# Value products behind two more product steps, a fourth bank for the first unit, an earlier tile, and a subtraction on another engine

## The chip, the cores and the metric

The kernel runs on one core of a Trainium2 chip. The core has a matrix engine (TensorE, PE in the profile), three engines for elementwise work (VectorE or DVE, ScalarE or ACT, GpSimd or POOL), and SyncE (SP), which only issues DMAs here. Each engine runs its own instructions in order and waits on semaphores for the others. Matrix products land in PSUM, which this kernel uses as eight banks of 128 x 512 fp32. The metric is the device time of one execution in microseconds.

## The reference

The output mixes sliding-window attention and a SwiGLU block, both of the same input, by a gate for each row:

```python
def _A_ref(x, wqkv, wo):                 # x: 1 x 2048 x 512
    H = 32; Dh = 16; W = 256
    q, k, v = split(x @ wqkv)            # 32 heads of 16
    scores = einsum("bhqd,bhkd->bhqk", q, k) * Dh ** -0.5
    mask = (i - j >= 0) & (i - j < W)    # the last 256 keys
    p = softmax(where(mask, scores, -1e9))
    return heads_joined(einsum("bhqk,bhkd->bhqd", p, v)) @ wo
def _B_ref(x, w_gate, w_up, w_down):     # 512 -> 1792 -> 512
    return (silu(x @ w_gate) * (x @ w_up)) @ w_down
g = sigmoid((x * gate_w).sum(-1, keepdims=True))
out = g * _A_ref(x) + (1 - g) * _B_ref(x)
```

## The kernel before

**Precision.** Products of fp32 operands are made of halves: a tensor is split into a high part (a cast to the matrix engine's fp32 format) and a low part (the rest). `split(hi, lo, src, hi_eng, lo_eng)` issues the cast on one engine and the subtraction on another. Three products then make one: high x high, high x low, low x high (`mm3`, lines 80 to 82).

**Stages.** Up to about 165 us the input is split, and the values, queries, keys and the first part of the feed-forward products are made. Then runs the stage of this case, up to about 635 us: attention over eight groups of four heads, with the other feed-forward products dealt in between, so that TensorE has work while the softmax is on its way. From 635 us on comes the last stage: the down projection and the output projection of the attention.

**The dealt products.** A unit is a block of 128 rows of gate or up (`UNITS`), computed in four chunks of 512 tokens, twelve matmuls a chunk. `stream()` is a generator that yields after each step. The first unit goes through `whole` (L506) with one matmul of 128 rows a step. All others go through `lanes` (L527): there one step is two matmuls, one on the upper and one on the lower 64 rows of the array, which run side by side; the lower lane is `LAG` = 18 steps behind. When a chunk is complete, `copy_out` has ScalarE copy its bank to `ev` (L499) and a DMA store it in DRAM (`raws`).

**Banks.** `bank(name)` takes the banks of a name in turn. Each of `pa`, `pb`, `pc`, `pd` has two at first. For this stage `pb0` is added to `pa`, for the dealt products, and `pb1` to `pc`, so `pa` and `pc` have three.

**Attention.** A tick is one head of one block of 128 tokens. In a tick, `stage1` makes the scores of the next group for the row maximum (L560, into `pc`, read by VectorE L562), and `stage2` the transposed scores of this group (L599, into `pd`); ScalarE takes their exponential (L601), and GpSimd cuts the window's edges with two selects (L603, L606). Four blocks are a slot. Once in a slot, in the second tick (`hd == 1`) of its first block (`part == 0`), stand the value products of the slot before: `av` issues 96 matmuls (64 in the first slot of a group) on half the rows each (L621), alternating between two banks, the first from `pc`, the second from `pd`; in the last group both come from `pc`. Behind them, `evacuate` has ScalarE copy the second bank to `ob` (L632), VectorE copy the first to `oe` (L638), GpSimd add them (L639) and store them in DRAM (`od<-oe`, L640). In the last group VectorE does the sum itself (L634), and GpSimd only stores.

**How many steps stand where.** `DEAL` gives the number of steps of each of a slot's four blocks, (4, 9, 9, 8), and (9, 9, 9, 8) in the last group (`t >= g7`, where there is no stage 1). A block's number is dealt out over its four ticks as evenly as whole numbers allow, so the four of the first block are 1, 1, 1, 1. In a tick the order is: the scores, then the value products and `evacuate` if it is their tick, then the steps, then what the table `AT` holds for the end of that tick.

**The table `AT`.** `at(k, f)` has `f` run at the end of tick `k`; `later(n, f)` does so `n` ticks from now. In this way DMAs, splits and the early tiles get their place. `tile_early(n)` (L702 to L712) prepares tile `n` of the feed-forward block's hidden activations in six pieces: an exponential on ScalarE, an addition, a reciprocal and two multiplications on VectorE (L706 to L709), and the split, its cast on ScalarE and its subtraction on VectorE. The ticks for these six are given relative to tick 4 x (g7 + 10).

**The last stage's loads.** `load_wo(k)` issues the load of a quarter of `wo` and returns its split, with the cast on ScalarE and the subtraction on GpSimd (`act`). GpSimd's queue also issues the loads of the attention outputs (`load_oc`, L818) and of the softmax's inverse sums (`load_rd`, L823). VectorE multiplies the two (L830).

## Time and profile before

| | us |
|---|---|
| median of 3 runs (lowest, highest) | 838.55 (837.27, 838.75) |
| profiled execution | 840.86 |
| its span, first to last instruction | 839.2 |
| TensorE busy | 828.3 |
| VectorE busy | 552.9 |
| ScalarE busy | 475.1 |
| GpSimd busy | 403.0 |

The mean granted TensorE clock is 0.998 of full speed. The rows that the prediction quotes are of these kinds. A row of the timeline has the start in us, the duration, the engine, the line, the operation, and the tile it writes and the tiles it reads; `xN` stands for N like instructions in a row; in brackets is the idle time ahead of it and what ended it. A duration of a matmul is its time in the pipeline, and matmuls overlap, so the pitch is read from starts. A row of waits has the waiting engine, its tile and line, what released it, and then the total, the count and the largest. A row of windows has the stretch and its length, then the busy time of PE, weight loads, DVE, ACT and POOL, the granted clock, the DMA engines' busy share and GB/s.

### The profile page before, as it was taken

The page shows a single profiled execution, that of the slowest core. Times are in us where ns is not written, and L with a number is a line of the kernel's source. Part 1 is how long each engine was busy: PE and PEld are TensorE (multiplying, and loading weights), DVE is VectorE, ACT ScalarE, POOL GpSimd, SP SyncE. Part 2 cuts the span into 40 slices and gives each one's busy share as a digit, 9 for nine tenths or more (in the row PEclk, how much of TensorE's full clock was granted, in tenths as well). Part 3 has the DMA queues.
Part 4 walks back from the last instruction along what each step waited for, and adds up shares of the span by engine and source line. Part 5 has one row for each costly group of instructions (what it writes and reads, how often), then busy time and mean ns, then how long its engine had stood idle before and what let it go on. Part 6 is the DMA issues. An engine that isn't in the chain of part 4 may idle for free.

```text
span 839.2 us, 20503 instructions
## 1 busy us (share of the span) xinstructions
PE 828.3 (99%) x7681; PEld 702.7 (84%) x7681; DVE 552.9 (66%) x1420; ACT 475.1 (57%) x955; POOL 403.0 (48%) x717
## 2 busy tenths in 40 slices
PE   9999999999999999999999999999999999999997
PEld 7888888869988988989889888898877887888886
DVE  5675554238877887888878887685457657554652
ACT  7454553212576767767667676676776554434341
POOL 5124441340365666667666566565763234342220
PEclk9999999999999999999999999999999999999999
DMA  8456676483625555456554554532648878868611
GB/s 297 143 174 227 225 259 229 137 266 125 214 97 174 188 178 186 158 189 191 184 177 157 187 179 160 175 108 100 214 156 287 303 217 250 284 219 246 214 51 50
DMA packets 79844, 158.91 MB, mean 189 GB/s; under 512 B 14913, under 2 KB 19393, under 8 KB 79745
## 3 DMA queue, kind: packets, MB, share of 16 engines
q1 hardware_dynamic: 68256, 126.91, 46.4%
q0 software_dynamic: 10912, 29.65, 10.5%
q8 instruction: 60, 0.98, 0.5%
q10 hardware_dynamic: 576, 1.05, 0.4%
q14 instruction: 40, 0.32, 0.1%
HBM read 92.80 MB, written 64.75 MB: 188 GB/s over the span
## 4 chain that ended last, share of the span: by engine, by line
PE 93%; DMA 2%; DVE 1%; issue 1%; ACT 1%; SPq 1%; POOL 1%; DVEq 0%; ACTq 0%
PE pa L527 21%; PE pb L527 11%; PE pd L599 6%; PE pd L621 4%; PE pd L380 4%; PE pb L380 4%; PE pa L380 4%; PE pc L621 4%; PE pc L560 3%; PE pc L80 3%; PE pd L82 3%; PE pc L81 3%; PE pc L82 3%; PE pd L80 2%; PE pd L81 2%; PE pc L380 2%
## 5 line engine op out<-in xcount | busy, mean ns | idle before, releaser
L601 ACT ACTIVATE pt<-pd 128x384 f32<-128x384 f32 (+2 forms) x512 | 232.7, 473 | 50.6 <-PE pc L560 13.7
L562 DVE CUSTOM_DVE_ANT_0 pc<-pc,mask 128x384 f32<-128x384 f32 (+2 forms) x320 | 171.9, 547 | 32.4 <-PE pc L560 15.1
L599 PE MATMUL pd<-q,k 64*128 64x384 f32 (+2 forms) x512 | 170.7, 346 | 0.1
L527 PE MATMUL pa<-xlo,wh 64*128 64x512 f32 x488 | 160.1, 401 | 0.0
L527 PE MATMUL pa<-xhi,wh 64*128 64x512 f32 x488 | 159.7, 396 | 0.0
L527 PE MATMUL pa<-xhi,wl 64*128 64x512 f32 x488 | 157.6, 394 | 0.0
L603 POOL TENSOR_SCALAR_AFFINE_SELECT pt<-pt 128x256 f32<-128x256 f32 x256 | 110.7, 433 | 78.5 <-ACT pt L601 67.3
L560 PE MATMUL pc<-k,q 63*128 63x384 f32 (+2 forms) x320 | 103.8, 327 | 0.0
L599 PEld LDWEIGHTS pd<-q,k 64*128 64x128 f32 x512 | 92.8, 184 | 10.7 <-ACT pt L601 3.5
L527 PE MATMUL pb<-xlo,wh 64*128 64x512 f32 x248 | 99.6, 402 | 0.0
L527 PE MATMUL pb<-xhi,wh 64*128 64x512 f32 x248 | 98.3, 396 | 0.0
L527 PE MATMUL pb<-xhi,wl 64*128 64x512 f32 x248 | 97.4, 393 | 0.0
L562 DVE CUSTOM_DVE_ANT_0 pb<-pb,mask 128x384 f32<-128x384 f32 (+2 forms) x160 | 87.5, 547 | 14.6 <-PE pb L560 10.6
L606 POOL TENSOR_SCALAR_AFFINE_SELECT pt<-pt 128x256 f32<-128x256 f32 x224 | 91.5, 408 | 0.0
L527 PEld LDWEIGHTS pa<-xlo,wh 64*128 64x128 f32 x488 | 79.4, 186 | 4.3 <-issue 3.6
L527 PEld LDWEIGHTS pa<-xhi,wh 64*128 64x128 f32 x488 | 80.3, 186 | 2.2 <-DVE mx L562 0.5
L527 PEld LDWEIGHTS pa<-xhi,wl 64*128 64x128 f32 x488 | 79.6, 186 | 2.2 <-issue 0.2
L562 DVE DVE_READ_ACCUMULATOR2_ANT mx<- 128x1 f32 x512 | 72.4, 141 | 0.0
L867 DVE TENSOR_TENSOR sg<-got,sg 128x512 f32<-128x512 f32 x53 | 45.9, 867 | 38.9 <-ACT sg L866 33.1
L621 PE MATMUL pc<-pt,vg 64*32 64x320 f32 (+4 forms) x1120 | 63.1, 349 | 0.0
L621 PE MATMUL pd<-pt,vg 64*32 64x320 f32 (+4 forms) x1184 | 62.9, 346 | 0.0
L560 PEld LDWEIGHTS pc<-k,q 63*128 63x128 f32 x320 | 58.9, 185 | 3.0 <-issue 0.4
(302 smaller groups left out, 2040.9 us busy)
## 6 DMA issues: line engine op xcount, KB each, us to landing
got<-raws SPq DMA_DIRECT2D x106, 256.0 KB
raws<-ev SPq DMA_DIRECT2D x92, 256.0 KB
q<-xd SPq DMA_DIRECT2D x96, 128.0 KB
k<-xd SPq DMA_DIRECT2D x96, 128.0 KB
xd<-cx SPq DMA_DIRECT2D x16, 512.0 KB
xd<-cy SPq DMA_DIRECT2D x16, 512.0 KB
od<-oe POOLq DMA_DIRECT2D x32, 256.0 KB, 3.1
raw<-wgu SPq DMA_DIRECT2D x24, 256.0 KB
```

Of the source, the lines that this page charges most:

```text
L80: nc.tensor.matmul(ps, lh, rh, start=start and i == 0, stop=False, skip_group_check=skip)
L82: nc.tensor.matmul(ps, ll, rh, start=False, stop=stop and i == n - 1, skip_group_check=skip)
L380: nc.tensor.matmul(ps, l[:, w], r[:, k], start=n in (1, 2, 5) and k == m == 0, stop=k == 1 and m == 2, skip_group_check=True)
L527: mm = nc.tensor.matmul(ps[o], w[r], x[r], start=not lane and i == 0, stop=bool(lane) and i == 3 * NK - 1)
L560: nc.tensor.matmul(ps[:, :n], QT[g % 2][pr][r, q0:q0 + P], KT[g % 2][pr][r, k0:k0 + n], start=True, stop=True)
L562: mx = nc.vector.tensor_tensor_reduce(out=ps[:, :n], in0=ps[:, :n], in1=mask[:, 3 * P - n:], scale=1.0, scalar=NEG, op0=ALU.add, op1=ALU.m ...
L599: nc.tensor.matmul(ps[:, :n], KT[g % 2][pr][r, k0:k0 + P], QT[g % 2][pr][r, k0:k0 + n], start=True, stop=True)
L601: BEHIND.append(nc.scalar.activation(pt[:, j, :n], ps[:, :n], AF.Exp, scale=SCALE))
L603: nc.gpsimd.affine_select(out=pt[:, :, :P], in_=pt[:, :, :P], pattern=[[0, 2], [1, P]], compare_op=ALU.is_ge, fill=0.0, base=0, channel_mu ...
L606: nc.gpsimd.affine_select(out=pt[:, :, 2 * P:], in_=pt[:, :, 2 * P:], pattern=[[0, 2], [-1, P]], compare_op=ALU.is_ge, fill=0.0, base=-1, ...
L621: nc.tensor.matmul(AV[g, c][h][32 * j:32 * j + 32, q0 - c * CH:q1 - c * CH], VG[4 * g + kb // 4][o, kb % 4, 17 * j:17 * j + 32], PT[g, kb, ...
L867: nc.vector.tensor_tensor(out=sg, in0=gu[1], in1=sg, op=ALU.mult)
```

## The change

It has four parts.

The first unit gets a fourth bank: `pb1` belongs to `pa` while `whole(UNITS[0])` runs, and goes over to `pc` before the lanes begin.

In a slot's first block the four ticks are dealt 1, 2, 1, 0 steps (outside the last group), and in every tick the steps now stand ahead of the value products and of `evacuate`. On TensorE, the second tick of a slot's first block before (names: `pa` to `pd` banks with their use's number; `pt` exponentials, `vg` values, `q`, `k` queries and keys; `xhi`, `xlo`, `wh`, `wl` the halves of input and weights; two L527 are a step):

```order
L560 MATMUL pb_3597<-k_1365,q_1345 128x384
L599 MATMUL pd_3600<-q_1501,k_1503 128x384
L621 MATMUL pc_3605<-pt,vg 32x320
L621 MATMUL pd_3606<-pt,vg 32x320
...
L527 MATMUL pa_3594<-xlo_97,wh 128x512
L527 MATMUL pb_3445<-xlo_93,wh 128x512
L560 MATMUL pc_3672<-k_1413,q_1387 128x384
L599 MATMUL pd_3676<-q_1513,k_1515 128x384
L527 MATMUL pa_3594<-xhi_96,wl 128x512
L527 MATMUL pb_3445<-xhi_92,wl 128x512
```

And now:

```order
L562 MATMUL pc_3597<-k_1365,q_1345 128x384
L601 MATMUL pd_3600<-q_1501,k_1503 128x384
L527 MATMUL pa_3594<-xlo_97,wh 128x512
L527 MATMUL pa_3445<-xlo_93,wh 128x512
L527 MATMUL pa_3594<-xhi_96,wl 128x512
L527 MATMUL pa_3445<-xhi_92,wl 128x512
L623 MATMUL pb_3609<-pt,vg 32x320
L623 MATMUL pd_3610<-pt,vg 32x320
...
L562 MATMUL pc_3674<-k_1413,q_1387 128x384
L601 MATMUL pd_3678<-q_1513,k_1515 128x384
L527 MATMUL pa_3594<-xhi_96,wh 128x512
L527 MATMUL pa_3445<-xhi_92,wh 128x512
```

Two steps stand between the scores and the value products, and directly behind the products come the next tick's scores.

Early tile 0's split comes at tick 10 instead of 14 of its table; tile 1's exponential at 4 instead of 7, its four operations of VectorE at 8 instead of 14, its split at 14 instead of 23. On VectorE, in the second half of the last group, before (`ev` the tile's working copy, `oe` the sum of two value banks, `den` the softmax's sums):

```order
L708 TENSOR_TENSOR ev<-k_1515,ev 128x512
L709 TENSOR_TENSOR ev<-k_1515,ev 128x512
L634 TENSOR_TENSOR oe<-pc_9979,ob 128x512
L457 RECIPROCAL den<-den 128x128
L71 TENSOR_TENSOR k_1503<-ev,k_1503 128x512
L706 TENSOR_SCALAR ev<-ev 128x512
L707 RECIPROCAL ev<-ev 128x512
L708 TENSOR_TENSOR ev<-q_1501,ev 128x512
L709 TENSOR_TENSOR ev<-q_1501,ev 128x512
```

And now:

```order
L710 TENSOR_TENSOR ev<-k_1515,ev 128x512
L711 TENSOR_TENSOR ev<-k_1515,ev 128x512
L708 TENSOR_SCALAR ev<-ev 128x512
L709 RECIPROCAL ev<-ev 128x512
L710 TENSOR_TENSOR ev<-q_1501,ev 128x512
L711 TENSOR_TENSOR ev<-q_1501,ev 128x512
L636 TENSOR_TENSOR oe<-pb_9988,ob 128x512
L71 TENSOR_TENSOR k_1503<-ev,k_1503 128x512
L457 RECIPROCAL den<-den 128x128
```

Tile 1's four operations moved ahead of the sum `oe` of a slot's value banks, which stood ahead of them.

The subtractions of `wo`'s split go from GpSimd to VectorE. On GpSimd at the start of the last stage, before (`raw` is what is loaded of `wo`, `xhi` the places that `od` and `rd` are loaded to):

```order
L806 DMA raw_10532<-wo 128x512
L71 TENSOR_TENSOR wol<-raw_10482,woh 128x512
L806 DMA raw_10559<-wo 128x512
L71 TENSOR_TENSOR wol<-raw_10507,woh 128x512
L818 DMA xhi_90<-od 128x1x512
L71 TENSOR_TENSOR wol<-raw_10532,woh 128x512
L823 DMA xhi_94<-rd 128x1x512
L71 TENSOR_TENSOR wol<-raw_10559,woh 128x512
L818 DMA xhi_90<-od 128x1x512
```

And now:

```order
L808 DMA raw_10532<-wo 128x512
L808 DMA raw_10559<-wo 128x512
L820 DMA xhi_90<-od 128x1x512
L825 DMA xhi_94<-rd 128x1x512
L820 DMA xhi_90<-od 128x1x512
L825 DMA xhi_94<-rd 128x1x512
L455 DMA den<-od 128x1x128
```

The loads stand one behind the other, with no subtraction between them. The new lines shift the numbers: from `stream` on, a line of the kernel before has 2 more in the changed kernel.

```diff
-        BANKS["pc"].append("pb1")
+        BANKS["pa"].append("pb1")
...
             yield from whole(UNITS[0])
+            BANKS["pa"].remove("pb1")
+            BANKS["pc"].append("pb1")
...
-        for n, ticks in enumerate(((2, 5, 5, 5, 5, 14), (7, 14, 14, 14, 14, 23))):
+        for n, ticks in enumerate(((2, 5, 5, 5, 5, 10), (4, 8, 8, 8, 8, 14))):
...
-        DEAL = (4, 9, 9, 8), (9, 9, 9, 8)
+        DEAL = [[[(hd + 1) * n // 4 - hd * n // 4 for hd in range(4)] for n in deal] for deal in ((4, 9, 9, 8), (9, 9, 9, 8))]
+        DEAL[0][0] = 1, 2, 1, 0
...
+                if t < G * NB:
+                    run(steps, DEAL[t >= g7][part][hd])
                 if hd == 1 and values:
                     av(*divmod(d - 1, NCH))
                     while UNDER:
                         UNDER.pop(0)()
                     evacuate(*divmod(d - 1, NCH))
-                if t < G * NB:
-                    n = DEAL[t >= g7][part]
-                    run(steps, (hd + 1) * n // 4 - hd * n // 4)
                 tick_end()
...
-            return lambda: split(woh[:, k], wol[:, k], raw, *act)
+            return lambda: split(woh[:, k], wol[:, k], raw, nc.scalar, nc.vector)
```

## The prediction, made before the result was known

> **What bounds the kernel now.** I read the page first (span, busy time, the chain of waits), then TensorE's waits, then the timeline at each place where the change acts.
>
> ```profile
> span 839.2 us, 20503 instructions
> PE 828.3 (99%) x7681; PEld 702.7 (84%) x7681; DVE 552.9 (66%) x1420; ACT 475.1 (57%) x955; POOL 403.0 (48%) x717
> PE 93%; DMA 2%; DVE 1%; issue 1%; ACT 1%; SPq 1%; POOL 1%; DVEq 0%; ACTq 0%
> ...
> PE pd L82 <- DVE hl L71: 1.7, 1, 1.7
> PE pa L506 <- ACT ev L499: 1.5, 1, 1.5
> PE pc L80 <- ACT ob L632: 1.4, 1, 1.4
> ```
>
> TensorE is busy for 99% and carries 93% of the chain. Its large visible idle places (total, count, largest) are worth 1.4 to 1.7 us each, and three of the four edits aim at these three. A busy PE can still hide waits: matmuls overlap, and a product waiting for its bank can count as busy, so for the slots I read starts of matmuls, not idle time. The work in TensorE is the same before and after; only waits can change. The sum is made against the profiled execution, 840.86 us with its span of 839.2; the median of the runs shown is 838.55, 2.31 less, and I carry the difference over to it. About 0.2% (1.68 us) is what a measurement of this kernel can tell from no change.
>
> **Part A, the first unit in four banks.** Rows of the timeline (start, duration, then the wait in brackets) and of the windows (sum; busy PE, weight loads, DVE, ACT, POOL; granted clock; DMA share):
>
> ```profile
> 174.69 1.07 ACT L499 COPY ev<-pa 128x512 f32<-128x512 f32 x2 [6.81 <-DMA q<-xd]
> 175.33 0.50 PE L506 MATMUL pa<-xhi,wh 128*128 128x512 f32 x1 [1.49 <-ACT ev L499]
> ...
> 173.59:177.00 3.41, 1.92 (x9) 1.15 (x8) 1.02 (x7) 1.56 (x3) 2.93 (x4) 1.00 0.80 265
> 177.00:180.42 3.42, 3.42 (x9) 2.12 (x9) 0.96 (x6) 0.00 (x0) 0.00 (x0) 0.50 0.82 257
> ...
> 181.00 0.39 PE L527 MATMUL pa<-xhi,wh 64*128 64x512 f32 x1
> 181.23 0.39 PE L527 MATMUL pa<-xlo,wh 64*128 64x512 f32 x1
> ```
>
> The fourth chunk finds no free bank: it waits for ScalarE's copy of the first, and ScalarE stands behind a DMA until 174.69. PE idles 1.49 us, and 1.67 us later the clock is at 0.50 for one stretch of 3.42 us. With one bank more the chunk needs no copy. From 175.33 to the first lane matmul at 181.00 are 5.67 us. Unhindered, the twelve products at 0.23 each (the pitch from 181.00 to 181.23) and three pairs of scores between them, about a pitch or a little more each, take 2.75 + 0.8 = 3.55. Of the 2.12 too many, 1.71 is half of the stretch at half clock. So the lanes begin about 173.85 + 3.55 = 177.4 in place of 181.0: **-3.6**. If ordinary runs don't lose the clock there, it is -1.9 (1.49 and 0.4): the ends are -3.6 and -1.9, and I take the one that this execution shows. The bank comes from `pc`, which has none to miss until the lanes start, and it is handed back before that.
>
> The Trainium skill ("TensorE: Matmul & The Clock Gate", Part 1: The HAM clock gate) has the clock fall after an idle window of about 3.4 us. The stretch here has that length, but the idle ahead of it was 1.49 us, so the measurement decides: a shorter gap can do it.
>
> **Part B, value products behind two more steps.** A slot's starts in a group with banks `pc` and `pd`, and then a last-group slot, where stage 1 is absent and both banks are free:
>
> ```profile
> 295.06 0.34 PE L599 MATMUL pd<-q,k 64*128 64x384 f32 x1
> 295.33 0.72 PE L621 MATMUL pc<-pt,vg 64*32 64x320 f32 x2
> 295.66 0.45 PE L621 MATMUL pd<-pt,vg 64*32 64x320 f32 x1
> 297.93 0.27 PE L621 MATMUL pd<-pt,vg 64*32 64x128 f32 x1
> 298.96 0.44 PE L599 MATMUL pd<-q,k 64*128 64x384 f32 x1
> 299.42 0.44 PE L599 MATMUL pd<-q,k 64*128 64x384 f32 x1
> ...
> 298.32 0.59 ACT L632 COPY ob<-pd 128x512 f32<-128x512 f32 x1 [2.33 <-PE pd L621]
> 298.88 1.57 ACT L601 ACTIVATE pt<-pd 128x384 f32<-128x384 f32 x3
> ...
> 308.40 0.72 PE L621 MATMUL pb<-pt,vg 64*32 64x320 f32 x2
> 308.97 0.45 PE L621 MATMUL pd<-pt,vg 64*32 64x320 f32 x1
> 311.23 0.27 PE L621 MATMUL pd<-pt,vg 64*32 64x128 f32 x1
> ...
> 607.76 0.45 PE L621 MATMUL pc<-pt,vg 64*32 64x320 f32 x1
> 610.04 0.27 PE L621 MATMUL pb<-pt,vg 64*32 64x128 f32 x1
> ```
>
> From the first start to the last the 96 products took 2.60 us in the first slot, 2.83 in the second, 2.28 in the last group. The excess (0.32 and 0.55) stands at the second product: its `pd` bank is held by scores until their exponential is out. Two steps ahead of the products give that time. They cost PE 2 x 0.23 = 0.46 ahead; the wait pays back 0.32 in a slot like the first (net +0.14) and all of it in one like the second (0 to -0.08).
>
> Behind the products those two steps are gone, and this is no gain: the score matmul at 298.96 starts as the copy of the value bank ends (298.32 + 0.59 = 298.91), and the next one at 299.42 as the first exponential ends (298.88 + about 0.5), so both are set by ScalarE and the PE work between filled a wait. By the slot's place in its half: 7 slots with +0.14, 6 at about +0.1 (their wait lies between), 14 at about -0.08 make 1.0 + 0.6 - 1.1, about **+0.4**. Ends: -1 if the middle ones gain as well, and +12 if no wait is saved (27 x 0.46); the last-group row, where banks are free and the products wait for nothing, speaks for the low end.
>
> **Part C, early tile sooner.** The places:
>
> ```profile
> 622.94 0.77 DVE L709 TENSOR_TENSOR ev<-k,ev 128x512 f32<-128x512 f32 x1
> 624.27 0.69 DVE L634 TENSOR_TENSOR oe<-pc,ob 128x512 f32<-128x512 f32 x1 [0.56 <-ACT ob L632]
> 629.59 0.42 DVE L706 TENSOR_SCALAR ev<-ev 128x512 f32<-128x512 f32 x1
> 630.04 3.35 DVE L707 RECIPROCAL ev<-ev 128x512 f32<-128x512 f32 x1
> 634.15 0.69 DVE L709 TENSOR_TENSOR ev<-q,ev 128x512 f32<-128x512 f32 x1
> ...
> 625.26 0.56 POOL L640 DMA_DIRECT2D od<-oe  x1 [2.09 <-DVE oe L634]
> 625.26:633.30 8.04, 8.04 (x70) 5.92 (x74) 5.19 (x4) 6.14 (x17) 8.00 (x18) 1.00 0.62 200
> 632.88 0.42 POOL L603 TENSOR_SCALAR_AFFINE_SELECT pt<-pt 128x256 f32<-128x256 f32 x1
> ...
> 634.75 0.27 PE L621 MATMUL pc<-pt,vg 64*32 64x128 f32 x1
> 637.97 0.50 PE L80 MATMUL pc<-q,k 128*128 128x512 f32 x1 [1.35 <-ACT ob L632]
> ```
>
> The aim is the 1.35 us at 637.97: ScalarE's copy of the last value bank stands behind the split of early tile 1, whose DVE operations end at 634.84. Written earlier, these four (629.59 to 634.84, 5.26 us) now stand on VectorE directly behind tile 0's last, which ends at 623.71, and ahead of the add L634 that began at 624.27. So that add ends not at 624.96 but near 623.71 + 5.26 + 0.69 = 629.7. GpSimd's store `od<-oe` waits for it and starts near 630.0 instead of 625.26; behind the store GpSimd has 8.04 us without a gap (busy 8.00 of 8.04) up to the last select, which then ends at 638.0 instead of 633.30. The last value products need that select. Of them only the last block is left by then, about 0.4: 638.4. Six products into `pd` at 0.23 (1.38) and the change of place bring the first into `pc` to 640.0, where it stood at 637.97: **+2.0**, and +3.0 if the products take their whole 1.45 (633.30 to 634.75) after it. PE then idles some 2.2 us, longer than the 1.49 of part A that a half clock followed; that costs between nothing and 1.71, and I take 1.2, nearer to the row that fell: **+3.2** in all. Worked as meant, without GpSimd's delay, it would be -1.35.
>
> By the Trainium skill (the same page, "Why this matters for your kernels") only gaps in TensorE over about 3 us cost the clock; then the 1.2 goes and part C is +2.0. Part A's row speaks against it.
>
> The idle 1.35 and 1.72 us at 637.97 and 698.91 passed without such a stretch, and that is why I don't take the full 1.71.
>
> **Part D, `wo`'s low halves on VectorE.**
>
> ```profile
> 665.19 1.28 POOL L71 TENSOR_TENSOR wol<-raw,woh 128x512 fp32r<-128x512 f32 x1 [15.97 <-ACT woh L68]
> 682.26 0.65 POOL L823 DMA_DIRECT2D xhi<-rd  x1
> ...
> 665.62 1.40 DVE L867 TENSOR_TENSOR sg<-got,sg 128x512 f32<-128x512 f32 x1 [0.36 <-ACT sg L866]
> 696.96 0.69 DVE L830 TENSOR_TENSOR raw<-xhi,xhi 128x512 f32<-128x512 f32 x1 [5.79 <-issue]
> 698.91 0.50 PE L82 MATMUL pd<-q,hl 128*128 128x512 f32 x1 [1.72 <-DVE hl L71]
> ```
>
> GpSimd's four subtractions wait for ScalarE's casts, and behind them stand the loads of `od` and `rd`. The last is issued at 682.26; VectorE's division waits 5.79 us for it until 696.96, and what VectorE owes TensorE then comes 1.72 late. Moved off, GpSimd issues all eight loads without those waits. The first of them alone held it for 15.97 us, more than the 5.79 by which the load came late: the stall goes, **-1.7**. VectorE takes four subtractions, 4 x 0.69; against them its own operation at 665.62 took 1.40 beside GpSimd's, twice the 0.69 of the same size at 696.96, so I count 0. If that doubling has another cause, the 2.8 us lie under VectorE's idle time (66% busy); without that cover they would delay PE by at most 2.8. Ends -1.7 and +1.1.
>
> **Sum:** -3.6 + 0.4 + 3.2 - 1.7 = -1.7: span 837.5, execution 839.1, and from the median 838.55 - 1.7 = **836.8**.
>
> **Rivals.**
> - *C without the clock's loss*, as the idle 1.35 us at 637.97 had none: -2.9, 835.6. Chance 0.11. The Trainium skill's section on gaps speaks for it.
> - *C as meant*: GpSimd's queue turns out to have slack, or the reciprocal finds its input late and the add slips in front. -3.6 + 0.4 - 1.35 - 1.7 = -6.25: 832.3. Against it: the order of the two operations on VectorE is fixed, and GpSimd's 8.00 of 8.04. 0.10.
> - *Slower, by part B alone*: the banks are still not free when the products come, or ScalarE's chain behind them is late by what they lost, at 0.2 us a slot: 27 x 0.2 = +5.4 instead of +0.4, +3.3 in all, 841.8. For it: ScalarE sets both matmuls behind the products, so any shift lands on PE in full. From 0.14 a slot (+3.8) the whole is slower than 840.2. 0.25.
> - *A's wait stays in another form* (the lanes' first banks wait for the same late copies): +1.9, 840.4. 0.07.
> - *B gains*, 0.1 a slot: -4.8, 833.7. 0.05.
> - The forecast: 0.42, with 835 to 839 of its own.
>
> **Numbers.** Faster than 836.87: 0.22 of the forecast's 0.42, 0.09, 0.10, 0.05, together 0.46. Within 0.2%: 0.17, 0.02, 0.05 (B) and 0.02 (A), 0.26. Slower than 840.23: 0.03, 0.20, 0.05, 0.28. The range 833.0 to 842.0 leaves out C as meant and the worse part of B's loss, some 0.18.
>
> **What would show it.** A: no idle at the fourth chunk, clock 1.00 after it, first lane matmul near 177.4. B: first and second value product 0.01 apart, 2.28 us from first to last; from one slot's first score matmul to the next slot's the same time as before, within 0.14. C: on VectorE the add behind the second reciprocal, GpSimd's store near 630 less what A gained, a PE wait for a select or for the last value products of some 4 us around 634 to 638, perhaps a stretch at 0.50. D: the last `rd` load issued before 675 and no PE wait at the division. The forecast falls if slots differ by more than 0.14 us, if the last select is not late, or if the half clock in A belongs to this one execution.

## The result: slower by 0.4%

The changed kernel takes 841.20 us (median of 7 runs, 840.38 to 843.89) where the kernel before takes 838.55 (7 runs, 837.27 to 839.49): a ratio of 1.0037, 95% interval 1.0023 to 1.0051 (the ratio is estimated from all the runs of both, so it is not exactly that of the two medians). The forecast was 836.8 and faster; the time lies in its range, but on the other side of no change.

The profiled execution of the changed kernel took 843.89 us and is the longest of its seven, as that of the kernel before (840.86) was longer than all its seven. The page's span, busy time and chain of waits, and then TensorE's largest waits, without one in the first microseconds that both kernels have:

```profile
span 842.2 us, 20499 instructions
PE 830.5 (99%) x7681; PEld 700.5 (83%) x7681; DVE 548.5 (65%) x1424; ACT 471.3 (56%) x955; POOL 398.9 (47%) x713
PE 96%; DMA 1%; POOL 1%; SPq 0%; ACT 0%; DVE 0%; issue 0%; DVEq 0%; ACTq 0%
...
PE pc L623 <- POOL pt L605: 2.0, 1, 2.0
PE pd L80 <- ACT hh L68: 1.6, 1, 1.6
...
PE pd L82 <- DVE hl L71: 0.9, 1, 0.9
```

The three waits that the change aimed at are gone (1.7 for the attention's low halves, 1.5 in the first unit, 1.4 for the last copy). Three others stand there, all at the end of the attention stage or just behind it. The windows show where the time went, first the kernel before, then the changed one (stretch and length; busy PE, weight loads, DVE, ACT, POOL; clock; DMA share and GB/s):

```profile
166.00:182.00 16.00, 14.51 (x59) 10.20 (x58) 2.90 (x16) 3.29 (x6) 10.52 (x12) 0.89 0.81 264
630.00:660.00 30.00, 28.65 (x213) 22.85 (x213) 22.14 (x32) 19.03 (x36) 7.56 (x16) 1.00 0.94 333
660.00:700.00 40.00, 38.28 (x170) 31.39 (x169) 20.10 (x28) 20.21 (x35) 13.66 (x19) 1.00 0.78 224
```

```profile
166.00:182.00 16.00, 16.00 (x77) 12.12 (x75) 4.91 (x23) 3.29 (x6) 11.84 (x13) 1.00 0.84 267
630.00:660.00 30.00, 25.35 (x185) 18.78 (x184) 14.05 (x23) 15.25 (x28) 10.71 (x23) 0.94 0.84 296
660.00:700.00 40.00, 40.00 (x177) 32.90 (x176) 22.40 (x37) 22.56 (x40) 6.51 (x11) 1.00 0.92 254
```

The first stretch (part A) and the third (part D) lose nothing any more, neither idle time nor clock. Between 630 and 660 (part C) PE's idle time rises from 1.35 to 4.65 us and the clock falls to 0.94. Read along the instructions of TensorE, the changed kernel is 3.2 us ahead at the first lane matmul, 2.2 at the start of the last group, 1.3 at the start of the last value products, 2.0 us behind at their end, 4.85 behind some fifty products later, and 3.0 behind from the attention's first output products on, to the end.

**Part A in the trace.** The first lane matmul has moved from 181.00 to 177.76:

```profile
177.76 0.39 PE L527 MATMUL pa<-xhi,wh 64*128 64x512 f32 x1
```

**Part B.** The slot whose first value product stood at 295.33 before, on PE and then on ScalarE:

```profile
292.59 0.45 PE L623 MATMUL pb<-pt,vg 64*32 64x320 f32 x1
292.59 0.45 PE L623 MATMUL pd<-pt,vg 64*32 64x320 f32 x1
294.87 0.27 PE L623 MATMUL pd<-pt,vg 64*32 64x128 f32 x1
295.95 0.44 PE L601 MATMUL pd<-q,k 64*128 64x384 f32 x1
296.35 0.44 PE L601 MATMUL pd<-q,k 64*128 64x384 f32 x1
...
295.32 0.58 ACT L634 COPY ob<-pd 128x512 f32<-128x512 f32 x1 [2.53 <-PE pd L623]
295.80 1.58 ACT L603 ACTIVATE pt<-pd 128x384 f32<-128x384 f32 x3
```

Both banks now start together, and the 96 products take 2.28 us (292.59 to 294.87) instead of 2.60. Behind them the score matmuls start 1.08 and 1.48 us after the last value product; before it was 1.03 and 1.49, with one step more ahead of the first and two more ahead of the second. So the steps taken from there were indeed free.

**Part C.** VectorE, GpSimd and TensorE at the end of the stage:

```profile
626.16 0.69 DVE L711 TENSOR_TENSOR ev<-q,ev 128x512 f32<-128x512 f32 x1
626.77 0.68 DVE L636 TENSOR_TENSOR oe<-pb,ob 128x512 f32<-128x512 f32 x1
627.97 0.95 DVE L457 RECIPROCAL den<-den 128x128 f32<-128x128 f32 x1
...
627.75 0.56 POOL L642 DMA_DIRECT2D od<-oe  x1 [7.34 <-DVE oe L636]
636.03 0.42 POOL L605 TENSOR_SCALAR_AFFINE_SELECT pt<-pt 128x256 f32<-128x256 f32 x1
...
634.84 0.40 PE L623 MATMUL pc<-pt,vg 64*32 64x256 f32 x1 [1.96 <-POOL pt L605]
636.50 0.24 PE L623 MATMUL pb<-pt,vg 64*32 64x64 f32 x1 [0.26 <-POOL pt L605]
```

GpSimd's store waits 7.34 us for the sum behind tile 1's operations, and its selects are late with it. The value products wait 1.96 us for one of them in their middle, and 0.26 us more for the last, which ends at 636.45. This is the mechanism that the prediction named. Then comes what it did not name. The chain of waits behind the last value product (start, duration, what), the ScalarE operation and the PE rows that wait, and the clock:

```profile
637.13 0.32 SPq L863
...
637.50 1.82 SPq L863
...
639.37 0.43 SPq L863
...
639.84 7.30 DMA got<-raws
...
645.81 0.63 ACT L868 ACTIVATE sg<-got 128x512 f32<-128x512 f32 x1 [4.13 <-DMA got<-raws]
647.00 0.50 PE L80 MATMUL pd<-q,hh 128*128 128x512 f32 x1 [1.58 <-ACT hh L68]
648.59 0.80 PE L82 MATMUL pd<-q,hl 128*128 128x512 f32 x1 [0.85 <-DVE hl L71]
649.00:652.40 3.40, 3.40 (x10) 2.63 (x10) 1.94 (x4) 2.07 (x4) 0.00 (x0) 0.60 0.99 300
```

SyncE loads the stored halves of the feed-forward products into `got`. The first of these loads goes out as the last value product ends, before (635.10, product ends 635.02) as after (637.13 and 637.03). The fourth, from 639.84 on, takes 7.30 us. GpSimd's batch, which begins with the last `od<-oe` (638.70) and goes on with one store and three loads, is on the DMA engines at that time. ScalarE waits 4.13 us for the third. In the kernel before that same operation had nothing to wait for:

```profile
639.80 0.63 ACT L866 ACTIVATE sg<-got 128x512 f32<-128x512 f32 x1
```

The rows of GpSimd's store, before and now:

```profile
639.06 0.56 POOL L640 DMA_DIRECT2D od<-oe  x1 [5.77 <-DVE oe L634]
...
638.70 0.56 POOL L642 DMA_DIRECT2D od<-oe  x1 [2.25 <-DVE oe L636]
```

Before, it began 4.0 us behind the last value product; now it begins 1.7 us behind it, because the copy of the bank no longer stands behind a late cast and the silu that follows this cast on ScalarE.

**Part D.** VectorE at the attention's first division, and GpSimd's loads for it:

```profile
696.04 0.94 DVE L457 RECIPROCAL den<-den 128x128 f32<-128x128 f32 x1
696.90 0.63 DVE L832 TENSOR_TENSOR raw<-xhi,xhi 128x512 f32<-128x512 f32 x1
...
672.15 0.63 POOL L825 DMA_DIRECT2D xhi<-rd  x1
678.53 0.59 POOL L825 DMA_DIRECT2D xhi<-rd  x1 [0.51 <-DMA xhi<-od]
```

The division follows the reciprocal without a wait, and PE passes 660 to 700 without any idle time.

### The profile page after: what moved, and what is told of

It is laid out like the page before. It is cut to its first block, busy times and chain, and to the rows that moved or that the text cites. A ratio compares the mean times of both kernels' runs of the same rounds, so it can differ in the third digit from the quotient of the medians.

```text
span 842.2 us, 20499 instructions
## 1 busy us (share of the span) xinstructions
PE 830.5 (99%) x7681; PEld 700.5 (83%) x7681; DVE 548.5 (65%) x1424; ACT 471.3 (56%) x955; POOL 398.9 (47%) x713
## 4 chain that ended last, share of the span: by engine, by line
PE 96%; DMA 1%; POOL 1%; SPq 0%; ACT 0%; DVE 0%; issue 0%; DVEq 0%; ACTq 0%
PE pa L527 22%; PE pb L527 11%; PE pd L601 7%; PE pc L623 4%; PE pd L380 4%; PE pb L380 4%; PE pa L380 4%; PE pc L562 4%; PE pd L82 3%; PE pc L81 3%; PE pc L82 3%; PE pc L80 3%; PE pd L81 3%; PE pd L80 3%; PE pd L623 2%; PE pb L623 2%
## 5 line engine op out<-in xcount | busy, mean ns | idle before, releaser
L601 PE MATMUL pd<-q,k 64*128 64x384 f32 (+2 forms) x512 | 175.1, 357 | 0.7 <-ACT ob L634 0.3
L527 PE MATMUL pa<-xlo,wh 64*128 64x512 f32 x496 | 161.8, 396 | 0.0
L527 PE MATMUL pa<-xhi,wl 64*128 64x512 f32 x496 | 160.2, 392 | 0.0
L527 PE MATMUL pa<-xhi,wh 64*128 64x512 f32 x496 | 159.4, 396 | 0.1
L562 PE MATMUL pc<-k,q 63*128 63x384 f32 (+2 forms) x322 | 105.9, 333 | 0.0
L527 PE MATMUL pb<-xlo,wh 64*128 64x512 f32 x240 | 94.8, 395 | 0.0
L527 PE MATMUL pb<-xhi,wh 64*128 64x512 f32 x240 | 94.6, 394 | 0.0
L527 PE MATMUL pb<-xhi,wl 64*128 64x512 f32 x240 | 94.2, 393 | 0.0
L527 PEld LDWEIGHTS pa<-xhi,wl 64*128 64x128 f32 x496 | 81.9, 185 | 1.7
L527 PEld LDWEIGHTS pa<-xhi,wh 64*128 64x128 f32 x496 | 79.9, 186 | 3.6 <-ACT pt L603 1.1
L527 PEld LDWEIGHTS pa<-xlo,wh 64*128 64x128 f32 x496 | 80.8, 185 | 1.3
L869 DVE TENSOR_TENSOR sg<-got,sg 128x512 f32<-128x512 f32 x53 | 41.8, 788 | 49.1 <-ACT sg L868 39.6
L641 POOL TENSOR_TENSOR oe<-oe,ob 128x512 f32<-128x512 f32 (+1 forms) x28 | 35.0, 1251 | 55.0 <-ACT ob L634 50.9
```

Source lines behind the costliest of these rows:

```text
L527: mm = nc.tensor.matmul(ps[o], w[r], x[r], start=not lane and i == 0, stop=bool(lane) and i == 3 * NK - 1)
L562: nc.tensor.matmul(ps[:, :n], QT[g % 2][pr][r, q0:q0 + P], KT[g % 2][pr][r, k0:k0 + n], start=True, stop=True)
L601: nc.tensor.matmul(ps[:, :n], KT[g % 2][pr][r, k0:k0 + P], QT[g % 2][pr][r, k0:k0 + n], start=True, stop=True)
```

## The experiments

All times are medians. The runs were measured in several series, each with runs of the kernel before beside it, and the ratio is to those. The kernel before stood at 838.50 to 839.27 in these series, and its single runs spread from 836.9 to 844.9.

| run | us | ratio to before | 95% interval |
|---|---|---|---|
| the change | 841.20 | 1.0037 | 1.0023 to 1.0051 |
| tile_back (A, B, D) | 837.15 | 0.9974 | 0.9960 to 0.9989 |
| deal_back (A, C, D) | 839.43 | 0.9997 | 0.9979 to 1.0015 |
| banks_alone (A) | 837.26 | 0.9978 | 0.9961 to 0.9994 |
| wo_alone (D) | 836.93 | 0.9967 | 0.9954 to 0.9981 |
| banks_and_wo (A, D) | 835.83 | 0.9954 | 0.9939 to 0.9968 |
| tile_behind_add | 842.91 | 1.0037 | 1.0024 to 1.0050 |
| cast_at_23 | 840.99 | 1.0022 | 1.0003 to 1.0041 |
| cast_at_23_ops_at_8 | 840.80 | 1.0025 | 1.0010 to 1.0039 |
| ops_at_11 | 836.68 | 0.9966 | 0.9950 to 0.9982 |
| wd_on_sync | 839.60 | 1.0009 | 0.9997 to 1.0021 |
| ops_at_11_wd_on_sync | 835.97 | 0.9966 | 0.9953 to 0.9979 |
| silu_behind_copy | 834.79 | 0.9944 | 0.9921 to 0.9966 |
| one_step_ahead | 834.29 | 0.9936 | 0.9912 to 0.9961 |
| one_step_ops_at_11 | 833.98 | 0.9932 | 0.9911 to 0.9953 |
| one_step_silu | 833.78 | 0.9941 | 0.9922 to 0.9960 |
| one_step_silu_wd_on_sync | 833.32 | 0.9938 | 0.9920 to 0.9956 |

### The parts apart

**tile_back**: the changed kernel, part C undone.

```diff
-        for n, ticks in enumerate(((2, 5, 5, 5, 5, 10), (4, 8, 8, 8, 8, 14))):
+        for n, ticks in enumerate(((2, 5, 5, 5, 5, 14), (7, 14, 14, 14, 14, 23))):
```

> The changed kernel with the early tiles' ticks of before; the other three parts stay. Theory: the early tile is what made the change slow, by about 6 us in two places (the last value products 3.3 us longer, then the last stage's first hidden activations 4.5 us late, less 1.65 us of the old wait there). So the last value products run 2.28 us as before, and what is left is -3.2 (banks), +1.2 (deal) and -2.0 (wo): about -4.0 us, 834.5. Rival: the late activations of the last stage come of the loads that part D issues earlier or of everything being earlier; then they stay, and the time is near 839.

Measured 837.15, 4.05 us below the change. The last value products take 2.35 us, and no wait stands at the first hidden activations (the first products of the last stage that need `got`), so both losses of 630 to 660 come of part C; the rival falls. The gain is smaller than expected (834.5): in the profiled execution the span is 3.8 us shorter than before, but ordinary runs of the kernel before are shorter than its profiled one.

**banks_alone** and **wo_alone**: the kernel before with part A or part D alone.

```diff
         BANKS["pa"].append("pb0")
-        BANKS["pc"].append("pb1")
+        BANKS["pa"].append("pb1")
...
             yield from whole(UNITS[0])
+            BANKS["pa"].remove("pb1")
+            BANKS["pc"].append("pb1")
```

> The kernel before with the first unit in four banks and nothing else. Theory: the first lane matmul stands at 177.8 instead of 181.0 and all behind it 3.2 us earlier, so 835.3. Rival: the half clock there belongs to the profiled executions, and ordinary runs gain 1.9 us or less, 836.7.

Measured 837.26, 1.6 us less than before (838.86), with single runs from 836.3 to 839.9. In the profiled execution, the shortest of its ten, the lanes begin 3.6 us earlier, and the wait of part D, which this kernel still allows, does not occur. The median fits the rival: ordinary runs of the kernel before mostly do not lose the stretch at half clock. The mean granted clock of every run bears this out. A stretch like that of the profiled execution costs 0.002 of it (1.7 of 839 us). Of the 96 runs of the kernel before that stand beside these experiments, 23 have 0.998 or less (840.09 to 844.85 us); the other 73 have 0.999 or 1.000 (836.94 to 840.25).

```diff
-            return lambda: split(woh[:, k], wol[:, k], raw, *act)
+            return lambda: split(woh[:, k], wol[:, k], raw, nc.scalar, nc.vector)
```

> The kernel before with wo's subtractions on VectorE and nothing else. Theory: the 1.72 us at the attention's first low halves go, and 2.0 with what follows, in every execution: 836.9. Rival: in ordinary runs the loads come early enough in most executions, as they did in the profiled one of the four banks alone, where this wait was absent; then -0.5 us, 838.3, with fewer of the long runs.

Measured 836.93, 2.1 us less than the 839.06 of the kernel before in that series. The theory holds. The profiled execution shows the same stage 2.0 us shorter. It shows something else too. Its first unit is that of the kernel before, and still, in the same two windows in which the prediction read the half clock, it shows these rows:

```profile
173.59:177.00 3.41, 2.58 (x12) 1.67 (x11) 1.22 (x8) 1.57 (x3) 3.02 (x4) 1.00 0.84 261
177.00:180.42 3.42, 3.42 (x19) 2.27 (x18) 1.75 (x8) 1.10 (x2) 0.51 (x1) 1.00 0.84 271
```

PE waits 0.83 us there instead of 1.49, the clock stays at 1.00, and the first lane matmul stands at 178.84 instead of 181.00, without any edit to that stage. So half of the 4.1 us by which this profiled span is shorter (839.2 to 835.1) is luck of the two executions, and not part D. The changed kernel's 177.76 is 1.1 us ahead of this.

**banks_and_wo**: parts A and D together.

> The kernel before with two parts of the change, the four banks and the subtractions of wo on VectorE. Theory: these two are all that gains, and the deal costs 0.73 us over its 27 slots and 0.25 in the last group, as the run with the tile's ticks of before showed; so this ends 1.0 to 1.2 us ahead of that run (837.15), at 836.0. Rival: the deal's loss is given back at the end of the stage, where a wait of 1.7 us stood in that run and 1.35 in the kernel before; then 836.6 or more.

Measured 835.83, as the theory had it. Its seven runs lie between 835.73 and 835.89, where those of the kernel before in that series spread from 837.51 to 842.23. This is not the work of both parts alike: wo_alone's ten runs already lie between 836.60 and 837.31, none with a clock below 0.999, while two of banks_alone's ten stand at 839.82 and 839.92 with 0.997. So the long runs seem to belong to the wait of part D rather than to that of part A; with ten runs each this is likely, not shown. Against wo_alone of the same series part A is worth 1.1 us; against tile_back part B costs 1.3 by the medians (the two series' medians of the kernel before differ by 0.2).

**deal_back**: the changed kernel, part B undone (the diff of the change, backwards).

> The changed kernel with the deal of before (1, 1, 1, 1 and the steps behind the value products); the other three parts stay. Theory: the deal costs 0.035 us a slot over 27 slots and some 0.25 in the last group, so this is 1.2 us faster than the changed kernel, about 840.0, and the slots show 2.60 and 2.83 us from first to last value product again. Rival: the last group's loss of 0.9 us (-2.25 to -1.3 against before) belongs wholly to the deal; then 1.9 us faster, 839.3.

Measured 839.43, 1.8 us less than the change. The time is near the rival's, but in the trace the rival's reason fails. From the first lane matmul to the last group this run keeps its lead over the kernel before (3.1 and 3.0 us), while the change loses 1.0 there. In the last group it loses 0.6 itself, against 0.95 in the change, so only a part of that loss belongs to the deal. The rest is the last stage, where the late loads cost this profiled execution 1.1 us and that of the change 4.5.

### What the early tile held

**tile_behind_add**: the changed kernel, with the sum ahead of tile 1's operations on VectorE.

```diff
-        for n, ticks in enumerate(((2, 5, 5, 5, 5, 10), (4, 8, 8, 8, 8, 14))):
+        for n, ticks in enumerate(((2, 5, 5, 5, 5, 10), (4, 9, 9, 9, 9, 14))):
```

> The changed kernel with tile 1's four VectorE operations one tick later (9 for 8), which on VectorE puts one instruction, the sum of the value banks, ahead of them and changes nothing else in the order of any engine. Theory 1: GpSimd's queue held behind that sum is the whole cause; then the last value products run 2.28 us, the first silu of the last stage does not wait, and the time is -4.0 - 1.35 = -5.4 us, 833.2. Theory 2: GpSimd's last store goes out early in any case, since ScalarE's copy no longer waits, and its batch of stores and loads gets ahead of SyncE's loads; then the first waits go, but the wait of 1.6 us and more at the last stage's first hidden activations stays, and the time is 836 to 838.

Measured 842.91, with the same ratio as the change, so no faster; both theories fall. ScalarE, PE and two windows of this run:

```profile
628.51 0.62 ACT L68 CAST q<-ev 128x512 fp32r<-128x512 f32 x1 [2.31 <-DVE ev L711]
629.47 0.79 PE L527 MATMUL pa<-xhi,wh 64*128 64x512 f32 x1 [2.06 <-ACT pt L603]
628.00:632.00 4.00, 2.53 (x9) 2.15 (x10) 2.49 (x4) 2.31 (x6) 1.75 (x5) 0.67 0.04 16
632.00:636.00 4.00, 4.00 (x19) 2.69 (x25) 0.00 (x0) 1.22 (x5) 3.99 (x9) 0.50 0.66 168
```

The cast of tile 1 stands ahead of four pairs of exponentials on ScalarE and now waits 2.31 us for VectorE, whose operations the sum pushed back. PE waits 2.06 us for an exponential, and then runs at half clock. So a second queue was held, ScalarE's. In the change the same cast waited 0.37 us only.

**cast_at_23** takes the casts back to their old ticks as well, and **cast_at_23_ops_at_8** (the second added line) then puts the operations ahead of the sum again.

```diff
-        for n, ticks in enumerate(((2, 5, 5, 5, 5, 10), (4, 8, 8, 8, 8, 14))):
+        for n, ticks in enumerate(((2, 5, 5, 5, 5, 14), (4, 9, 9, 9, 9, 23))):
...
+        for n, ticks in enumerate(((2, 5, 5, 5, 5, 14), (4, 8, 8, 8, 8, 23))):
```

> The changed kernel with the two splits of the early tiles at their ticks of before (14 and 23) and tile 1's VectorE operations at 9, so behind the sum of the value banks; tile 1's exponential and operations still come earlier than before. Theory: two queues were held by part C, GpSimd's behind the sum on VectorE and ScalarE's behind the cast of tile 1, and neither is here; the last value products run 2.28 us, the cast is ready when its turn comes, and the 1.4 to 1.7 us wait for the copy of the last value bank goes: 835.6, 1.5 faster than with the tile's ticks of before (837.15). Rival: GpSimd's store and its batch then go out 1.6 us behind the last value product and get ahead of SyncE's loads, and the first hidden activations are late: 837 to 839.

> As the run with the casts at their old ticks, but tile 1's VectorE operations at 8, ahead of the sum of the value banks: on VectorE one instruction has another place, and nothing else. Theory: this alone holds GpSimd for some 5 us, the last value products run about 5.6 us instead of 2.28 with a wait for a select of 2 us, and the time is 3 to 5 us above the other run, 839 to 841. Rival: ScalarE's early cast was what delayed the exponentials and through them the selects; then both runs are within 1 us of each other.

Measured 840.99 and 840.80: no difference, and the first is not the 835.6 of the theory. GpSimd and VectorE of cast_at_23 show why:

```profile
623.78 0.56 POOL L642 DMA_DIRECT2D od<-oe  x1 [3.52 <-DVE oe L636]
629.82 0.56 POOL L458 DMA_DIRECT2D rd<-den  x1 [4.17 <-DVE den L457]
...
628.58 0.95 DVE L457 RECIPROCAL den<-den 128x128 f32<-128x128 f32 x1
```

The store `od<-oe` is in time (623.78, where it stood at 625.26 before), but a few instructions on GpSimd stores `rd<-den`, the inverse sums of the softmax, and waits 4.17 us for a reciprocal that also stands behind tile 1's operations. So either of the two can hold the queue. In the change the sum came last, and it alone did: there `rd<-den` starts at 630.04 without a wait.

**ops_at_11** moves the operations behind this reciprocal too; on VectorE one instruction has another place than in cast_at_23, and no other engine's order differs.

```diff
-        for n, ticks in enumerate(((2, 5, 5, 5, 5, 14), (4, 9, 9, 9, 9, 23))):
+        for n, ticks in enumerate(((2, 5, 5, 5, 5, 14), (4, 11, 11, 11, 11, 23))):
```

> As the run with the casts at their old ticks, but tile 1's VectorE operations at 11 instead of 9: on VectorE the reciprocal of the softmax's sums (den) now stands ahead of them, and nothing else changes its place on any engine. Theory: in that run GpSimd's queue was held by its store of these inverse sums, which waited 4.2 us for the reciprocal, and by nothing else; so here the last value products run 2.28 us with no wait for a select, and as tile 1 is ready early the wait for the copy of the last value bank goes too: 5 us faster than that run (840.99) and 1 to 1.5 faster than with all the tile's ticks of before (837.15): 835.6 to 836.2. Rival: what made all runs with an early tile slow is VectorE itself, 5 us of work in front of ScalarE and GpSimd at the end of the stage, wherever it is put; then this stays above 839.

Measured 836.68, 4.3 us less than cast_at_23. The last value products take 2.55 us and have no wait, and PE no longer waits for the copy of the last bank. So the held queue was the cause, and VectorE is not the bound. But against tile_back (837.15) the early tile brings only 0.5 us where 1 to 1.5 was expected. VectorE and GpSimd, then the chain of waits and ScalarE of the profiled execution:

```profile
623.43 0.94 DVE L457 RECIPROCAL den<-den 128x128 f32<-128x128 f32 x1
625.63 0.56 POOL L458 DMA_DIRECT2D rd<-den  x1
...
636.55 9.36 DMA got<-raws
...
644.98 0.63 ACT L868 ACTIVATE sg<-got 128x512 f32<-128x512 f32 x1 [4.28 <-DMA got<-raws]
```

One of SyncE's loads takes 9.36 us. The 1.6 us won at the copy are lost again at the hidden activations, and 1.1 us more, in this profiled execution, the longest of its ten runs; nothing is held on an engine there. Once the copy is early, GpSimd's batch is early (2.0 us behind the last value product), and the loads are late.

### The loads that share the DMA engines

**wd_on_sync**: the changed kernel, with the two loads of `wd` in GpSimd's last batch issued by SyncE behind its first six loads. **ops_at_11_wd_on_sync** does the same to ops_at_11.

```diff
-        for f, (i, name) in enumerate(((13, "raw"), (13, "wh"), (13, "wl"), (17, "wh"), (17, "wl")), 8):
+        for f, (i, name) in enumerate(((13, "raw"), (13, "wh"), (13, "wl")), 8):
...
             load_kept(*loads.pop(0))
+        for f, name in ((11, "wh"), (12, "wl")):
+            WDRAW[f] = ring.tile([P, D], F32, name=name, bufs=2)
+            nc.sync.dma_start(WDRAW[f], wd[f])
```

> The changed kernel with the two loads of wd that follow GpSimd's last store issued by SyncE behind its first six loads of the stored halves; the store and the raw halves' store stay on GpSimd. Theory (the two queues share the DMA engines): with two transfers of 256 KB less beside it, SyncE's third load lands in 5 us or less where it took 6.4, the wait of 1.6 us for the first hidden activations falls below 0.6, and with it the stretch at half clock goes: 1.5 to 3 us faster than the changed kernel, 838.2 to 839.7. Rival: SyncE's third load is late for its own start (0.7 us behind the store, 2 us later than before), not for what runs beside it; then the wait stays, and so does the time, 841.

> The run with tile 1's operations at 11 (836.68, 836.5 its profiled span), and the two loads of wd behind GpSimd's last store issued by SyncE behind its first six loads of the stored halves. In that run the 1.6 us at the copy of the last value bank were won, and then TensorE waited 1.7 us for the first halves of a hidden activation, whose load had taken 8.9 us. Theory (GpSimd's batch shares the DMA engines with SyncE's loads): with two of its transfers put behind them, no load of the first six takes over 6 us, the wait goes, and the time is 1 to 2 us lower, 835.2. Rival: the store of the value sums and of the raw halves, which stay ahead, are what delays them; then within 0.5 us of 836.7.

Measured 839.60, 1.6 us less than the change, and 835.97, 0.7 less than ops_at_11. In the first, PE's waits for the hidden activations are gone; in the second they fall from 1.7 and 0.5 us to a single 1.4. The first points to the theory, though there SyncE's third load also went out ahead of GpSimd's store, not behind it. The second does not show a gain: against the kernel before of its own series it stands at 0.9966, as ops_at_11 does. That GpSimd's batch delays the loads is likely by these runs, and not shown to be all of it.

**silu_behind_copy**: parts A and D, and the third tile's silu, with its table load, behind the copy of the last value bank.

```diff
-                if t == G * NB and hd == 0:
-                    last_tile = tile_silu(2)
-                    run(last_tile, 1)
...
                     evacuate(*divmod(d - 1, NCH))
+                if t == G * NB and hd == 1:
+                    last_tile = tile_silu(2)
+                    run(last_tile, 1)
```

> Banks and wo as in the run with these two, and the third tile's silu with its table load behind ScalarE's copy of the last value bank instead of ahead of it; the early tiles stay as before. So GpSimd is not held anywhere, and only the wait for that copy goes. Theory (two queues collide): GpSimd's last store then goes out some 1.6 us behind the last value product instead of 4.0, its batch of five transfers gets ahead of SyncE's loads of the stored halves, the third of them lands after 5 us instead of 3, and the first hidden activations are late: the 1.4 us are won and lost again, and the time is that of banks and wo within 0.7 or up to 2 more. Rival (the late loads came of the held value products alone): 1.4 us faster than banks and wo, 834.6.

Measured 834.79, 1.0 us less than banks_and_wo. This is nearer to the rival: in the profiled execution the products behind the copy start 1.8 us earlier against banks_and_wo, and this is kept. GpSimd's store went out 2.1 us behind the last value product here, so an early batch is not enough for the loss. SyncE had issued four of its loads by then, and two in the change, but this does not decide it either: four were out in one_step_silu too, which lost 2.0 us at the hidden activations, and two in cast_at_23, which lost 0.4.

Over all eighteen profiled executions, the kernel before and the change among them, what TensorE loses at the hidden activations, read from the starts of its products against the kernel before, is 0 in the six where the store went out 4.0 to 4.2 us behind the last value product, and between 0 and 4.5 us in the twelve where it went out 1.7 to 2.3 us behind it. So an early batch goes with the loss; what sets its size stays open.

### One step in place of two

**one_step_ahead**: parts A and D, with one step of 1, 1, 1, 1 ahead of the value products, in all groups but the last.

```diff
+                if t < g7:
+                    n = DEAL[t >= g7][part]
+                    run(steps, (hd + 1) * n // 4 - hd * n // 4)
                 if hd == 1 and values:
...
-                if t < G * NB:
+                if g7 <= t < G * NB:
                     n = DEAL[t >= g7][part]
                     run(steps, (hd + 1) * n // 4 - hd * n // 4)
```

> Banks and wo, with the steps ahead of the value products but dealt 1, 1, 1, 1 as before, and the last group as before. Theory: one step ahead (0.23 us) only fills a wait that is there in every slot (0.32 to 0.55), and the two steps behind are as free as the three were, since ScalarE sets the matmuls there; so nothing changes, within 0.03 us a slot and 0.5 in all. Rival: what stands ahead costs in proportion, half of what two steps cost, +0.4 us, most of it in the slots of the second and fourth kind.

Measured 834.29, 1.5 us less than banks_and_wo. Both fall: neither no change nor a cost, but a gain of about 0.05 us in each of the 27 slots. The slot of part B's rows (295.33 before) in this run:

```profile
291.71 0.45 PE L623 MATMUL pb<-pt,vg 64*32 64x320 f32 x1
291.82 0.45 PE L623 MATMUL pd<-pt,vg 64*32 64x320 f32 x1
294.09 0.27 PE L623 MATMUL pd<-pt,vg 64*32 64x128 f32 x1
```

From first to last it is 2.38 us, 0.22 less than the 2.60 of the kernel before, for one step of 0.23: what stands ahead is paid by the wait, as the theory said. The gain comes behind: the second score matmul stands 1.41 us after the last value product instead of 1.49, so there two steps fit where three had just not.

**one_step_silu**, **one_step_ops_at_11** and **one_step_silu_wd_on_sync** put the gains together.

> The two gains over banks and wo taken together: one step ahead of the value products (-1.5 us) and the third tile's silu behind the copy of the last value bank (-1.0 to -1.6). Theory: they act at different places and add up, so 833.0. Rival: the silu's gain brings GpSimd's batch forward to where SyncE's loads are, and a little earlier work in front of it tips it over; then 834.3 or more.

> Banks, wo and one step ahead of the value products (834.29), with the early tile as in the run beside this one. Theory: the 1.5 us at the copy of the last value bank come on top, 832.8, unless GpSimd's batch, then early, delays SyncE's loads of the stored halves. Rival: that delay gives them back, 834 or more, as it gave back half in the run with the silu moved.

> Banks, wo, one step ahead and the third tile's silu behind the copy of the last value bank (833.78), with the same two loads put on SyncE. There the silu's move had won 1.6 us at the copy and lost 2.0 again at the first hidden activations in the profiled execution. Theory: that loss goes or halves, 832.6. Rival: as above, no change, 833.8.

Measured 833.78, 833.98 and 833.32. With one_step_ahead's 834.29 these are four versions within 1 us, with intervals that overlap; each is 0.6 to 0.7% faster than the kernel before and, by the medians, 0.8 to 0.9% faster than the change. In the profiled execution of the first the 1.8 us won at the copy are lost again at the hidden activations (2.0), so the rival holds there; in that of the second 0.6 are lost. What the early copy can bring is mostly taken by the loads behind it.

## Why the prediction was wrong

By its terms, each with what it measured in ordinary runs (differences of medians above) and in the profiled executions. The rows of B and C set runs of different series side by side; taken from the kernel before of each series, B is +1.5 and C +4.4.

| term | forecast | ordinary runs | profiled |
|---|---|---|---|
| A | -3.6 | -1.1 (beside D) to -1.6 (alone) | -3.2 at the first lane matmul |
| B | +0.4 | +1.3 (837.15 - 835.83) | +1.2 |
| C | +3.2 | +4.05 (841.20 - 837.15) | +6.8 |
| D | -1.7 | -1.4 (beside A) to -2.1 (alone) | -2.0 |
| sum | -1.7 | +2.65 (841.20 - 838.55) | +3.0 |

**A, the step that failed first.** "I take the one that this execution shows." The mechanism is right: lanes at 177.76 where 177.4 was forecast, no idle time, clock 1.00. But the stretch at half clock is absent from most executions: at least 73 of 96 runs of the kernel before have no such loss, and wo_alone passes the same place at 1.00. The profiled run of the kernel before stood 2.3 us over the median, as the prediction itself says, and it still carried the full 3.6 to the median. The lower end, -1.9, was nearer, and the prediction had named this among the signs that it falls.

**C, the step that was incomplete.** The delay of the last value products and what follows at once was forecast at +2.0. Measured by the first products into `pc` and behind, where the change is 0.4 us behind the kernel before and tile_back 1.7 ahead of it, it is 2.1. The reading of VectorE's order and of GpSimd's gapless 8.04 us was right. Two things were missed. The sum was not the only operation behind tile 1's: the reciprocal of the inverse sums moved with it, was in plain sight in the order, and can hold GpSimd by itself (cast_at_23, ops_at_11), though in the change the sum did it first. And the end of the last value product is also the signal on which SyncE's loads of the last stage start, while the early copy sends GpSimd's batch out ahead: the forecast followed the delay to the first product into `pc`, and not to the loads behind it. That is worth 4.5 us in the profiled execution of the change: the waits of 1.58 and 0.85 us, and some 1.7 by the clock (0.60 over 3.4 us, and a part of the stretch ahead). In ordinary runs it is some 2 us, if 2.1 of the 4.05 are the delay. In the change's trace the half clock came there, and not behind the idle time at 634, where the forecast had it. In two other traces it did come where the forecast had it: at the same wait, of 2.10 us in cast_at_23 and of 1.94 us in wd_on_sync, the clock is 0.50 from 634.6 to 638.0 and from 636.4 to 639.8. That +3.2 came near +4.05 is in part luck: the 1.2 us for the clock stand where the late loads should have stood.

**B, mis-sized.** "7 slots with +0.14, 6 at about +0.1, 14 at about -0.08." Against banks_alone, from one slot's first score matmul to the next slot's, tile_back shows +0.11 in the first kind, +0.06 and +0.26 in turns in the second, and -0.07 in the third: together +0.7. The prediction's own three numbers make 0.5, which it put down as +0.4. The method holds, and the middle kind was too cheap. The last group adds 0.3 that the sum did not have. In one_step_ahead, which leaves the last group's order as it was, this loss is absent, so it is the steps' place there that costs; the two banks are free in that group, so a step ahead of them has no wait to fill.

**D** came as forecast: no wait at the division, the last load of `rd` for it issued at 678.53 (forecast: before 675), and -2.0 in the profiled execution for -1.7.

With A at -1.1, B at +1.3, C at +4.05 and D at -2.1 the sum is +2.15, near the +2.65 measured. Of the rivals none came true. "Slower, by part B alone" had the right sign, and with 841.8 nearly the time, by luck, since B cost less than 0.05 us a slot and not 0.2. "C as meant" is nearly what ops_at_11 makes of it, and there it is worth 0.5 us and not the 1.35 of the removed wait.

The Trainium skill ("TensorE: Matmul & The Clock Gate", section "Why this matters for your kernels") names gaps over about 3 us in TensorE as what costs the clock. The traces differ: 1.49 us before 175.33, and 2.06 us before 629.47 in tile_behind_add, were followed by half clock. And 1.96 us before 634.84 in the change were not, though 1.94 us at the same product in wd_on_sync were. So between 1.3 and 2.1 us these traces show both, and a sum should carry such a loss as a chance.

## What to carry to other kernels

When an operation is written earlier on an in-order engine, list everything that it is now ahead of, and for each of these who waits for it and what is queued behind that waiter; here a single short reciprocal that was passed cost 4.3 us by the medians (cast_at_23 against ops_at_11). A wait that is removed at a stage's end starts the next stage's transfers in another order, so follow the chain to the first product that needs a load. And a sum made in one profiled execution must not carry its rare losses, here a stretch at half clock, to the median of runs that mostly lack them.

## What was not expected of the hardware

The loads of 256 KB that SyncE issues at this place took between some 3 us and 9.36 us in the traces, the longest where GpSimd's batch was out early; that the batch is the reason is likely and not shown. And in tile_behind_add the clock stayed at half for some 10 us (0.50 in the window 632 to 636) although PE was busy all of that window, with matmuls on 64 of the array's 128 rows; in the kernel before it was back after 3.4 us. Why it stayed is open.
